# A branch hint over a general path, the flag of that branch written at the end, and a changed warm-up

## The chip, the core and the metric

The kernel runs on one core of a Trainium2 chip. The metric is device time in microseconds (us), lower is better. The core has five engines that run their own instruction streams: TensorE (PE, matmuls, with weight loads PEld listed apart), VectorE (DVE), ScalarE (ACT), GpSimd (POOL) and SyncE (SP), which here issues all DMAs.

## What is computed

Input `x` is 2048 rows of 512 in bf16. Two branches read it and a gate mixes them:

```
g   = sigmoid(sum(x * gate_w))                 # one number per row
q,k,v = x@wq, x@wk, x@wv                       # 32 heads of 16, 4 segments of 512 rows
a_dot = softmax(q k^T / 4 + causal mask) v     # inside a segment
a_mem = phi(q) M / (phi(q) z + 1e-6)           # M, z: sums of phi(k) v and phi(k) of earlier segments
a   = (sigmoid(beta) * a_mem + (1 - sigmoid(beta)) * a_dot) @ wo
b   = (gelu(x @ w_gate) * (x @ w_up)) @ w_down # hidden width 1792
out = g * a + (1 - g) * b
```

## The kernel before

All weights and the transposed x (`xT`) live in SBUF. Work is cut into units that each fill one PSUM bank: four matmuls of 128x512 for a projection (`u_q` L235, `u_k` L290, `u_v` L312, `u_gate` L356, `u_up` L377, `u_out` L409) or fourteen for a down projection (`u_down` L393), followed by one evacuation on VectorE. The attention runs in groups of four heads (`group_qk` L507): four logit matmuls on row tiles of 32 partitions, a ScalarE exponential, GpSimd masks on the diagonal blocks, and then `pv` (L540). The loop over 4 segments, 4 head blocks and 5 groups (L814 to L856) issues one group at a time and fills TensorE with units from queues until a planned time; the order is the one written out by this planner (`manual_schedule`, L575), each engine taking its instructions in program order.

The start: `load_inputs` (L118) issues x0 (the first 512 rows, into a slice of the buffer `G[1]`), then wk, wq, beta, wv and the rest on SP's queue. `warm_up` (L143) clears another slice of `G[1]` and runs nine matmuls of zeros into a bank nobody reads. `transpose_x0` (L149) transposes x0 on TensorE; its copies on VectorE and ScalarE fill `xT`. Then come three k units, four q units, four v units.

The fast path takes the exponential of the logits without subtracting the row maximum. That is safe only while the logits are small. Units `absmax` and `u_bound` (L184, L197) bound them from the largest entries of x, wq and wk; the op at L222 writes `safe`, one int32 that is 1 if the bound holds, in the middle of the run. At the end every engine loads that word into a register (L966) and branches (L967): if it is 0, the block `general()` (L908) computes everything anew with row maxima. With the given inputs `safe` is 1. Of the general block, PE has about 9,300 instructions, DVE 1,336, ACT 677, SP 87, POOL 16. Block order in the program before: the body, the short block of the usual case (each engine waits for its own outstanding work and jumps to the end), the general block, the end. So the usual case falls through the compare and then jumps over the general block. `preferred_fallthrough_block` at L967 decides that order. The `min_val` and `max_val` at L966 make SP also check the value (two short register instructions).

The last step of each segment, `u_out`, adds the two branches into a tile `osb` (L418, three buffers) and SP stores it to `out` (L423). The last segment's four stores are the last DMAs of the kernel. At the end SP waits for all DMA queues, all engines meet at a barrier, semaphores are cleared, and they meet again.

Of the kernel before, what the change touches and what calls it, by code (L numbers as in the profile page):

```python
# [11 lines left out]
ALU = mybir.AluOpType  # L12

P = 128
D = 512
H = 32
DH = 16
NSEG = 4
# [4 lines left out]
EXP_LIMIT = 80.0  # L23
NG = 3
NK = 3
BF = dt.bfloat16
# [18 lines left out]
def kernel(  # L45
# [15 lines left out]
    nc = tc.nc  # L61
# [5 lines left out]
    out2 = out[0]  # L67

    cpool = ctx.enter_context(tc.tile_pool(name="c", bufs=1))
    wk2 = ctx.enter_context(tc.tile_pool(name="wk2", bufs=2))  # L70
# [5 lines left out]
    def const(shape, dtype, name):  # L76
        return cpool.tile(shape, dtype, name=name, tag=name)
# [23 lines left out]
    G = [const([P, HS, L], BF, f"G{i}") for i in range(NG)]  # L101
# [10 lines left out]
    bound = const([1, 8], F32, "bound")  # L112
    safe = const([1, 1], dt.int32, "safe")

    def gen(name):
        return pgen.tile([P, 512], F32, name=name, tag="gen")
# [24 lines left out]
    zero = G[1][:, KT, :]  # L141

    def warm_up():  # L143
        nc.vector.memset(zero, 0.0)
        T = gen("warm")
        for i in range(9):
            nc.tensor.matmul(T[:, :], lhsT=zero[:, 0:P], rhs=zero, start=True, stop=True)

    def transpose_x0():  # L149
        for fc in range(FC):  # L150
            T = pgen.tile([P, 1024], BF, name="x0T", tag="gen")
            for kt in range(KT):
                nc.tensor.transpose(T[:, kt * P:(kt + 1) * P],
                                    x0[:, kt, fc * P:(fc + 1) * P], ident[:, :])
            if fc % 2 == 0:
                nc.vector.tensor_copy(xT[:, fc, 0:L], T[:, 0:512])  # L156
            else:
                nc.scalar.copy(xT[:, fc, 0:L], T[:, 0:512])
# [38 lines left out]
    def u_bound():  # L197
        def join():
            nc.vector.tensor_reduce(out=amax[:, 3:4], in_=amax[:, 3:12], axis=mybir.AxisListType.X,
                                    op=ALU.max)  # L200
            nc.vector.tensor_tensor(out=amax[:, 0:1], in0=amax[:, 0:1], in1=amax[:, 3:4],
                                    op=ALU.max)
            nc.vector.tensor_copy(amaxb[:, :], amax[:, 0:3])
            passed(0.0, 0.3)

        def spread():
            room_for_bank()
            T = gen("bT")
            for i in range(3):
                nc.tensor.matmul(T[0:1, i * P:(i + 1) * P], lhsT=amaxb[:, i:i + 1],  # L210
                                 rhs=ident[:, :], start=True, stop=True)
            nc.vector.tensor_reduce(out=bound[:, 0:3],
                                    in_=T[0:1, 0:3 * P].rearrange("p (i q) -> p i q", i=3),
                                    axis=mybir.AxisListType.X, op=ALU.max)
            passed(0.15, 0.6)

        def test():
            nc.vector.tensor_tensor(out=bound[:, 3:5], in0=bound[:, 1:3],
                                    in1=bound[:, 0:1].to_broadcast((1, 2)), op=ALU.mult)
            nc.vector.tensor_tensor(out=bound[:, 5:6], in0=bound[:, 3:4], in1=bound[:, 4:5],  # L220
                                    op=ALU.mult)
            nc.vector.tensor_scalar(out=safe[:, :], in0=bound[:, 5:6],  # L222
                                    scalar1=float(DH ** 0.5 * D * D), scalar2=EXP_LIMIT,
                                    op0=ALU.mult, op1=ALU.is_le)
            passed(0.0, 0.4)

        def f():
            later(1, join)
            later(3, spread)
            later(5, test)  # L230
        return 0.0, 0.0, f
# [20 lines left out]
    def later(n, f):  # L252
        due.setdefault(clock[0] + n, []).append(f)
# [155 lines left out]
    def u_out(s, qt):  # L409
        def f():  # L410
            T = gen("aT")
            oT = oTs[s]
            for fc in range(FC):
                nc.tensor.matmul(T[:, :], lhsT=oT[:, fc, qt * P:(qt + 1) * P], rhs=wo[:, fc, :],  # L414
                                 start=(fc == 0), stop=(fc == FC - 1))
                if fc < FC - 1:
                    yield MM512
            osb = wk2.tile([P, D], BF, name="osb", tag="osb", bufs=3)  # L418
            nc.vector.scalar_tensor_tensor(out=osb[:, :], in0=T[:, :],
                                           scalar=gct[:, s, qt:qt + 1],  # L420
                                           in1=tBs[(s, qt)][:, :], op0=ALU.mult, op1=ALU.add)
            q0 = s * L + qt * P
            nc.sync.dma_start(out2[q0:q0 + P, :], osb[:, :])  # L423
            return MM512
        return 4 * MM512, EVAC, f

# [149 lines left out]
    load_inputs()  # L576
    make_identity(nc, ident[:, :])
    warm_up()
    transpose_x0()
    setup_consts()  # L580
# [19 lines left out]
    def passed(pe, dve=0.0):  # L600
        backlog[0] = max(0.0, backlog[0] - pe) + dve
        t_pe[0] += pe
# [17 lines left out]
    def room_for_bank():  # L620


        if current:
            current[0][3][0] += 1
            while current and current[0][3][0] > 2:
                step()
# [76 lines left out]
    for i in range(NK, NSEG * NC8):  # L703
        s, c = i // NC8, i % NC8
# [8 lines left out]
    for i in range(NC8, NSEG * NC8):  # L713
        s, c = i // NC8, i % NC8
# [149 lines left out]
    fill_to(1e9)  # L864
    assert not any(st.q for st in streams)


    def phi_now(dst, src):
        e = wk2.tile([P, 2, L], BF, name="phe", tag="phe")
        a = wk2.tile([P, 2, L], BF, name="pha", tag="pha", bufs=1)  # L870
        nc.scalar.activation(e[:, :, :], src, AF.Exp)
        nc.vector.tensor_scalar(out=a[:, :, :], in0=src, scalar1=0.0, scalar2=1.0,
                                op0=ALU.max, op1=ALU.add)
        nc.vector.tensor_tensor(out=dst, in0=e[:, :, :], in1=a[:, :, :], op=ALU.min)
# [88 lines left out]
                for half in range(2):  # L963
                    run(u_M(s, half))

    ok = nc.values_load(safe[0:1, 0:1], min_val=0, max_val=1)  # L966
    with tc.If(ok == 0, preferred_fallthrough_block=False):  # L967
        general()
# [1 line left out]
_INS = ['A_x', 'A_wq', 'A_wk', 'A_wv', 'A_wo', 'A_beta', 'B_x', 'B_w_gate', 'B_w_up', 'B_w_down', 'gate_w']  # L970
# [26 lines left out]
```

## Time and profile before

| what | value |
|---|---|
| time, median of 3 runs | 292.79 us (292.26 to 293.21) |
| profiled execution, its own time | 293.84 us |
| its span in the profile | 292.0 us |
| TensorE busy | 282.9 us, 97% |
| VectorE, ScalarE, GpSimd busy | 74%, 69%, 28% |
| last matmul starts | 286.5 us |
| last output op on VectorE ends | 287.65 us |
| last store: issued, landed | 287.68, 290.39 us |
| barrier after the branch complete | about 291.3 us |

The span runs from the first instruction of the profile to the last. The profiled execution's time is 1.85 us longer than its span; what lies between is ahead of the first recorded instruction or behind the last. A row of the profile's group views gives a source line, an engine (a q behind the name means its sequencer: branches, loads of registers, waits), an operation, how often, shortest, median and longest duration in ns, and first and last start in us.

### The profile page before, as it was taken

To read this page: it belongs to the slowest core of one execution; us is meant where nothing else is said; L and a number is where in the kernel's file an instruction comes from. 1 tells how busy PE (TensorE), PEld (TensorE's weight loads), DVE (VectorE), ACT (ScalarE), POOL (GpSimd) and SP (SyncE) were. 2 spreads that over 40 slices of the span, in tenths; PEclk is the share of its full clock that TensorE was granted. 3 is DMA by queue.
4 is the path that set the end of the run, shared out by engine and by line. 5 is a ranking of instruction groups with operands and counts; after the bars stand their busy time and mean duration, and the time that the engine had idled before them with its cause. 6 is when DMAs were issued, how large, how long until landed. Compare 5 with 4: busy or idle time off the path is not lost.

```text
span 292.0 us, 6916 instructions
## 1 busy us (share of the span) xinstructions
PE 282.9 (97%) x2960; PEld 138.2 (47%) x2960; DVE 215.7 (74%) x422; ACT 200.7 (69%) x125; POOL 82.7 (28%) x140
## 2 busy tenths in 40 slices
PE   7899999999999999999999999999999999999992
PEld 4344445554444454545444454455544544544451
DVE  1788488777876869987878968988768567785453
ACT  3226877768897776776898785767748968777600
POOL 4000043344204334243410424242323033244300
PEclk9999999999999999999999999999999999999998
DMA  6989940200000000400000001033101000011002
GB/s 214 325 189 251 308 84 3 54 20 2 20 0 2 20 20 18 93 20 20 18 20 18 2 2 36 3 76 34 38 0 38 2 0 20 18 21 38 22 19 79
DMA packets 29444, 15.85 MB, mean 54 GB/s; under 512 B 21984, under 2 KB 28384, under 8 KB 29408
## 3 DMA queue, kind: packets, MB, share of 16 engines
q1 hardware_dynamic: 29408, 15.35, 21.0%
q8 instruction: 25, 0.41, 0.6%
q14 instruction: 11, 0.09, 0.1%
HBM read 8.14 MB, written 2.10 MB: 35 GB/s over the span
## 4 chain that ended last, share of the span: by engine, by line
PE 56%; DVE 3%; issue 0%; DVEq 0%
PE dT L397 14%; PE uT L381 10%; PE od L546 7%; PE gT L360 6%; PE lg L519 6%; PE aT L414 4%; PE kT L294 2%; PE vT L316 2%; PE qT L239 2%; PE mn L496 1%; PE MT L434 1%; DVE ktb L299 0%; DVE G L368 0%; DVE pha L271 0%; DVE o L556 0%
## 5 line engine op out<-in xcount | busy, mean ns | idle before, releaser
L525 ACT ACTIVATE pT<-lg 128x2048 bf16<-128x2048 f32 x80 | 150.1, 1876 | 57.1 <-PE lg L519 46.0
L536 POOL TENSOR_SCALAR_AFFINE_SELECT pT<-pT 128x512 bf16<-128x512 bf16 x128 | 79.5, 639 | 194.1 <-ACT pT L525 192.2
L381 PE MATMUL uT<-xT,wup 128*128 128x512 bf16 x224 | 62.3, 379 | 0.0
L360 PE MATMUL gT<-xT,wga 128*128 128x512 bf16 x224 | 60.2, 379 | 0.6 <-DVE G L368 0.4
L397 PE MATMUL dT<-wdn,G 128*128 128x512 bf16 x224 | 55.2, 379 | 0.2 <-DVE G L387 0.2
L546 PEld LDWEIGHTS <-pT 128*128 128x128 bf16 x1280 | 43.6, 96 | 17.7 <-issue 0.4
L546 PE MATMUL od<-V,pT 128*128 128x17 bf16 x1280 | 43.9, 170 | 0.0
L387 DVE TENSOR_TENSOR G<-uT,G 128x512 bf16<-128x512 f32 x56 | 38.3, 686 | 6.8 <-PE uT L381 6.4
L368 DVE CAST G<-gT 128x512 bf16<-128x512 f32 x42 | 28.8, 685 | 8.0 <-PE gT L360 7.7
L519 PE MATMUL lg<-QT,KT 32*128 32x384 bf16 (+3 forms) x512 | 31.7, 301 | 0.0
L360 PEld LDWEIGHTS <-wga 128*128 128x128 bf16 x224 | 19.7, 97 | 22.8 <-issue 5.5
L397 PEld LDWEIGHTS <-G 128*128 128x128 bf16 x224 | 19.5, 97 | 22.2 <-issue 3.9
L381 PEld LDWEIGHTS <-wup 128*128 128x128 bf16 x224 | 19.2, 97 | 20.8 <-issue 5.0
L402 DVE TENSOR_SCALAR tB<-dT,omg 128x512 bf16<-128x512 f32 x16 | 12.0, 750 | 19.9 <-PE dT L397 19.8
L519 PEld LDWEIGHTS <-KT 32*128 32x128 bf16 x512 | 8.9, 92 | 29.8 <-issue 29.5
L375 ACT ACTIVATE G<-G 128x3584 bf16<-128x3584 bf16 x6 | 18.8, 3182 | 0.0
L239 PE MATMUL qT<-xT,wq 128*128 128x512 bf16 x64 | 17.4, 379 | 1.1 <-DMA wq<-in_A_wq_dram 1.1
L552 DVE RECIPROCAL rden<-od 128x16 f32<-128x16 f32 x32 | 8.2, 256 | 13.7 <-PE od L546 13.4
L294 PE MATMUL kT<-xT,wk 128*128 128x512 bf16 x64 | 17.1, 380 | 0.3 <-DVE xT L156 0.3
L414 PE MATMUL aT<-wo,oT 128*128 128x512 bf16 x64 | 16.4, 379 | 0.5 <-DVE G L368 0.5
L316 PE MATMUL vT<-wv,xT 128*128 128x512 bf16 x64 | 16.4, 380 | 0.0
L366 ACT ACTIVATE G<-gT 128x512 bf16<-128x512 f32 x14 | 8.4, 598 | 9.7 <-PE gT L360 9.7
(81 smaller groups left out, 226.2 us busy)
## 6 DMA issues: line engine op xcount, KB each, us to landing
out_dram<-osb SPq DMA_DIRECT2D x16, 128.0 KB, 1.7
wga<-in_B_w_gate_dram SPq DMA_DIRECT2D x1, 1792.0 KB, 13.7
wup<-in_B_w_up_dram SPq DMA_DIRECT2D x1, 1792.0 KB, 8.7
wdn<-in_B_w_down_dram SPq DMA_DIRECT2D x1, 1792.0 KB, 10.3
G<-in_A_x_dram SPq DMA_DIRECT2D x1, 512.0 KB, 3.9
wk<-in_A_wk_dram SPq DMA_DIRECT2D x1, 512.0 KB, 4.8
wq<-in_A_wq_dram SPq DMA_DIRECT2D x1, 512.0 KB, 9.0
wv<-in_A_wv_dram SPq DMA_DIRECT2D x1, 512.0 KB, 9.7
```

The source lines that it names most:

```text
L239: nc.tensor.matmul(T[:, :], lhsT=wq[:, fc, c * P:(c + 1) * P], rhs=xT[:, fc, s * L:(s + 1) * L], start=(fc == 0), stop=(fc == FC - 1))
L294: nc.tensor.matmul(T[:, :], lhsT=wk[:, fc, c * P:(c + 1) * P], rhs=xT[:, fc, s * L:(s + 1) * L], start=(fc == 0), stop=(fc == FC - 1))
L360: nc.tensor.matmul(T[:, :], lhsT=wga[:, fc, hs * P:(hs + 1) * P], rhs=xT[:, fc, s * L:(s + 1) * L], start=(fc == 0), stop=(fc == FC - 1))
L368: nc.vector.tensor_copy(G[s % NG][:, hs, :], T[:, :])
L381: nc.tensor.matmul(T[:, :], lhsT=wup[:, fc, hs * P:(hs + 1) * P], rhs=xT[:, fc, s * L:(s + 1) * L], start=(fc == 0), stop=(fc == FC - 1))
L387: nc.vector.tensor_tensor(out=g, in0=T[:, :], in1=g, op=ALU.mult)
L397: nc.tensor.matmul(T[:, :], lhsT=G[s % NG][:, hs, qt * P:(qt + 1) * P], rhs=wdn[:, hs, :], start=(hs == 0), stop=(hs == HS - 1))
L414: nc.tensor.matmul(T[:, :], lhsT=oT[:, fc, qt * P:(qt + 1) * P], rhs=wo[:, fc, :], start=(fc == 0), stop=(fc == FC - 1))
L519: nc.tensor.matmul(lg[:, j, off:off + n], lhsT=KTm[pp][32 * j:32 * j + 32, (NC8 * s + c) % NK, kt * P:(kt + 1) * P], rhs=QT[32 * j:32 * j ...
L525: nc.scalar.activation(pT[:, :, :], lg[:, :, :], AF.Exp, scale=DH ** -0.5)
L536: nc.gpsimd.affine_select(out=v, in_=v, pattern=pat, compare_op=ALU.is_ge, fill=0.0, base=0, channel_multiplier=-1)
L546: nc.tensor.matmul(od[:, qq, j, 0:17], lhsT=t[:, j, o:o + P], rhs=V[s % 2][:, kt, 8 * c + 2 * j + p, 0:17], start=(kt == 0), stop=(kt == qq))
```

## The change

Four edits. (1) `tc.If` gets a label and lets the general block fall through, and the usual block is moved behind it; a branch hint "LikelyTaken" for that branch is given to TensorE, VectorE and ScalarE. In the built program the hint is one instruction on each of the three, at the very start of the body, ahead of the first zero matmul. SP and GpSimd have the same branch without a hint. (2) The op that writes `safe` goes from `u_bound` to the end of the body; in VectorE's stream it stands right behind the last segment's last output op. The value check on SP goes. (3) The last segment's `osb` is a slice of `G[1]` in place of a tile of the three-buffer pool, so those four ops do not wait for earlier stores. (4) The nine zero matmuls become six, followed by eight of 256 columns on column tiles of 32. TensorE's body has 11 instructions more (ten for the warm-up, one hint); otherwise each engine's order is as before.

```diff
     def warm_up():
         nc.vector.memset(zero, 0.0)
         T = gen("warm")
-        for i in range(9):
+        for i in range(6):
             nc.tensor.matmul(T[:, :], lhsT=zero[:, 0:P], rhs=zero, start=True, stop=True)
+
+        for i in range(8):
+            j = i % 4
+            nc.tensor.matmul(T[32 * j:32 * j + 32, 0:256], lhsT=zero[:, 32 * j:32 * j + 32],
+                             rhs=zero[:, 0:256], start=True, stop=True,
+                             tile_position=(0, 32 * j))
...
-            nc.vector.tensor_scalar(out=safe[:, :], in0=bound[:, 5:6],
-                                    scalar1=float(DH ** 0.5 * D * D), scalar2=EXP_LIMIT,
-                                    op0=ALU.mult, op1=ALU.is_le)
             passed(0.0, 0.4)
...
-            osb = wk2.tile([P, D], BF, name="osb", tag="osb", bufs=3)
-            nc.vector.scalar_tensor_tensor(out=osb[:, :], in0=T[:, :],
+            if s == NSEG - 1:
+
+                osb = G[(s + 1) % NG][:, qt, :]
+            else:
+                osb = wk2.tile([P, D], BF, name="osb", tag="osb", bufs=3)[:, :]
+            nc.vector.scalar_tensor_tensor(out=osb, in0=T[:, :],
...
-            nc.sync.dma_start(out2[q0:q0 + P, :], osb[:, :])
+            nc.sync.dma_start(out2[q0:q0 + P, :], osb)
...
+    tc.mark_branch_hint_location("safe", "LikelyTaken",
+                                 [mybir.EngineType.PE, mybir.EngineType.DVE,
+                                  mybir.EngineType.Activation])
...
-    ok = nc.values_load(safe[0:1, 0:1], min_val=0, max_val=1)
-    with tc.If(ok == 0, preferred_fallthrough_block=False):
+    nc.vector.tensor_scalar(out=safe[:, :], in0=bound[:, 5:6],
+                            scalar1=float(DH ** 0.5 * D * D), scalar2=EXP_LIMIT,
+                            op0=ALU.mult, op1=ALU.is_le)
+    ok = nc.values_load(safe[0:1, 0:1])
+    with tc.If(ok == 0, preferred_fallthrough_block=True, label="safe"):
         general()
```

## The prediction

> **What bounds the kernel now.** I read the page first (share of each engine), then the page's DMA part, then the views of lines 966, 967, 992 and 423, and last the timeline of TensorE's start.
>
> ```profile
> span 292.0 us, 6916 instructions
> PE 282.9 (97%) x2960; PEld 138.2 (47%) x2960; DVE 215.7 (74%) x422; ACT 200.7 (69%) x125; POOL 82.7 (28%) x140
> ...
> q8 instruction: 25, 0.41, 0.6%
> ...
> out_dram<-osb SPq DMA_DIRECT2D x16, 128.0 KB, 1.7
> ```
>
> TensorE is busy 97% of the span, so the body is TensorE's. The change touches only what lies before its first projection and after its last matmul (286.9 us). Queue q8 moved 25 packets of instructions, 16 KB each (0.41 MB / 25). From 286.9 to 292.0 no engine needs matmuls; that stretch is the branch. The views of lines 967, 966, 992 and 423, one row per engine (count, min/median/max ns, first and last start in us):
>
> ```profile
> L967 ACTq COMPARE_BRANCH  x2: 38/44/49, 275.0 to 276.4; - x2
> L967 POOLq COMPARE_BRANCH  x2: 38/42/45, 276.9 to 277.7; - x2
> L967 PEldq COMPARE_BRANCH  x2: 83/1806/3530, 285.7 to 287.1; - x2
> L967 DVEq COMPARE_BRANCH  x2: 51/53/55, 287.6 to 287.8; - x2
> L967 SPq COMPARE_BRANCH  x2: 38/48/57, 288.9 to 290.5; - x2
> ```
> ```profile
> L966 PEldq TENSOR_LOAD <-safe x1: 484/484/484, 285.1 to 285.1; - x1
> L966 DVEq TENSOR_LOAD <-safe x1: 546/546/546, 286.9 to 286.9; - x1
> L966 SPq TENSOR_LOAD <-safe x1: 498/498/498, 288.1 to 288.1; - x1
> ```
> ```profile
> L992 SPq DRAIN  x3: 7/7/13, 291.2 to 291.5; - x3
> L992 ACTq DRAIN  x2: 8/54/100, 278.9 to 291.5; - x2
> L992 PEldq DRAIN  x2: 8/40/73, 290.6 to 291.6; - x2
> L992 DVEq DRAIN  x2: 10/34/59, 290.9 to 291.5; - x2
> ```
> ```profile
> DMA to landing us min/median/max: 1.7/1.7/2.7
> ```
>
> The second COMPARE_BRANCH of each engine is its jump over the general path; its DRAIN at line 992 is the first instruction behind the jump. PE leaves at 287.05 and arrives at 290.64 (3.59 us), DVE at 287.79 and 290.92 (3.13), ACT at 276.42 and 278.94 (2.5). POOL and SP, whose general blocks are 16 and 87 instructions, need under 0.2. So three engines stall in the jump. The trace's transfer records show why: a 16 KB instruction packet starts at 288.23 and takes 0.92 us; 8 KB ones start at 277.3 and 289.06.
>
> The end barrier waits for the last to arrive: by semaphore events PE 290.73, DVE 290.99, **SP 291.26**. SP ends last, and for another reason: it waits for the last output. That DMA was issued at 287.68 and landed at 290.385, 2.70 us later, where the median is 1.7 (line above). Fifteen of its sixteen semaphore counts came by 289.62, fourteen of them by 289.38. The sixteenth belongs to eight packets of 1 KB that ran one after another from 289.14 to 289.90: one DMA engine, starting as the 16 KB instruction packet ended (288.23 + 0.92 = 289.15). So TensorE's stall costs through a collision with the last store, more than by itself. From the landing SP takes 0.88 to arrive, then the barriers 0.72 to 291.985.
>
> **The change, part by part.** The sum is made against the profiled execution: span 291.985, its own time 293.84, which is 1.05 over the median of the runs, 292.79. I carry the difference over.
>
> *Hint and order of blocks.* General code now falls through and the usual path is the taken branch, with a hint for PE, DVE and ACT. If a target is fetched while the body still runs, the stalls go and with them the packet at 288.23. Landing: 287.683 + 1.69 (issue to landing of the two stores before the collision: 285.09 to 286.78, 285.95 to 287.64) = 289.38, against 290.385: **-1.0 us**. If the fifteenth count, at 289.62, stays where it is: -0.77. I take -0.98, nearer the row of the undisturbed stores. SP's 0.88 and 0.72 behind it are unchanged; next to be late is SP itself, still.
>
> *Flag written last.* The op costs 142 ns (its row, at 189.3 us) and moves behind the last output op, which ends at 287.655. Flag there at about 287.83. Every engine's load of it (0.47 to 0.55) now waits for that: behind it on PE, ACT, DVE and POOL there is only the branch; on SP too, whose load starts at 288.07 anyway, since it issues the last store first. Loads end near 288.4, branches near 288.5; then an own-engine wait, a second branch and the drain, 0.3: PE, DVE, ACT and POOL arrive near 289, 1.2 us ahead of SP's 289.38 + 0.88 = 290.26. Cost 0. If a fetch still comes then, that cover is gone (first rival). POOL and SP have no hint; their targets are as near as before (16 and 87 instructions): 0. SP's two register instructions (0.19 and 0.02) go: it waits for the landing anyway, 0.
>
> *A new fetch.* Each jump is followed by a fetch of the next block 0.59 to 0.67 us after the drain starts (PE 290.64 and 291.315, DVE 290.92 and 291.505, ACT 278.94 and 279.556). With jumps near 288.5 these fall near 289.1 to 289.25; the last store's packets end at 289.03 on undisturbed DMA engines. It clears, by 0.1 to 0.2 us: second rival.
>
> *Last outputs into G.* The last segment's four ops no longer wait for a store to free osb. The fourth did wait: for a landing at 286.783, but TensorE's result came later (286.875). Gain 0, covered by 0.09. G's slice was last read long before: 0.
>
> *Zero matmuls.* The start, in order of time (start, length, idle before):
>
> ```profile
> 4.22 1.06 PE L147 MATMUL warm<-G 128*128 128x512 bf16 x2
> 5.07 1.69 PE L153 MATMUL x0T<-ident,G 128*128 128x128 bf16 x16
> 7.05 2.75 PE L294 MATMUL kT<-xT,wk 128*128 128x512 bf16 x12 [0.29 <-DVE xT L156]
> 10.95 1.47 PE L239 MATMUL qT<-xT,wq 128*128 128x512 bf16 x6 [1.15 <-DMA wq<-in_A_wq_dram]
> ```
>
> The nine zero matmuls start 0.427 apart; x0 has landed by 4.67, so the transposes start 0.36 later than they could. Six end at 1.3 + 6 x 0.427 = 3.86. Eight of 256 columns: one by one 8 x 0.213 = 1.71, or, if four column tiles run beside each other as the four row tiles of line 519 do (four matmuls of 512 columns in 0.39), 0.43. No row shows column tiles; I take 0.43. Transposes then start between 4.7 and 5.6, i.e. -0.35 to +0.5 against 5.07. The 1.15 us that TensorE waits for wq at 10.95 swallows all of it: **0**. In a run where wq lands earlier, up to -0.3 comes through. The hints themselves are three instructions at the start, some 0.05 each by the branches' rows, under the same cover.
>
> Sum: -0.98. Span 291.0, profiled time 292.86, median **291.8**; the forecast's own range is 291.4 (-0.98 and -0.3 from the start) to 292.05 (-0.77).
>
> **Rivals.**
> 1. *The hint does nothing; slower.* It stands some 5,960 TensorE instructions ahead of its branch. For it: no row shows a hint at work. Against: a block is fetched long before it is run (TensorE's last one ahead of the branch at 276.3, 10.8 us before its jump), so there is time in which the target could be fetched too. Then the late flag puts the fetch at the very end: PE branches at 288.47, drains 3.59 + 0.15 later at 292.2, arrives 292.3, end + 0.72 = 293.0, +1.03: **293.8**. It decides as soon as a stall exceeds 291.26 - 288.7 = 2.5 us; DVE's and PE's do. The Trainium skill speaks for this one: Runtime: NRT & Kernel Launch, Instruction fetch mechanics, says that prefetch is purely sequential and a taken branch out of the window forces a fetch. The trace agrees with the second half (3.59 us); on the first nothing here tells, and by it the time would be this rival's.
> 2. *The stalls go, the landing stays late.* The target's or the next block's fetch meets the last store after all: 0.2 us earlier than I put it and one DMA engine's last packets wait up to 0.92. Gain 0.06 to 0.4: **292.6**. For it: the fetch of 16 KB did this at 288.23. Against: the margin above. If the landing was late for another reason, the change doesn't do what it says: 292.8, counted here.
> 3. *The clock comes late.* Transposes run 107 ns apart at first and 56 from 6.4 us: full rate came there. With a gap before x0 and narrow tiles in place of full ones, it may come only after kT: 12 x 0.427 = 5.12 in place of 2.75, kT ends 1.2 us past 10.95. Net +0.2: **293.0**. If it comes at 9.8, kT ends near 10.9 and nothing is lost; that is why I hold it unlikely. The Trainium skill, TensorE: Matmul & The Clock Gate, Part 1 and Part 4, says that the clock is released after a busy window of some 3.4 us and that transposes do not count as busy, which speaks for it; the order of events here (1.3 to 6.4) does not contradict either half.
>
> **How the numbers follow.** Forecast 0.60, rival 1 0.18, rival 2 0.13, rival 3 0.09. 0.3% is 0.88 us, about what a measurement of this kernel can tell from no change. Most of the forecast lies beyond it (0.50), gains of 0.77 to 0.88 do not (0.10). Rival 2 is within; rival 3 mostly (0.06, else 0.03 slower); rival 1 mostly slower (0.16, 0.02 within). Faster 0.50, same 0.31, slower 0.19. The range runs from 291.3 to 293.1: it takes in rivals 2 and 3 and leaves out rival 1's 0.18.
>
> **What would show it.** Right: PE's and DVE's branch near 288.5 followed by a drain within 0.4 us; the last store landing 1.7 us after issue; SP last to the barrier near 290.3; no 16 KB instruction packet between 287 and 289; first qT matmul still waiting for wq near 10.9. Wrong: a branch of over 2 us after 288.4 (rival 1); prompt drains but a landing over 2.2 us (rival 2); kT matmuls 0.427 apart, or qT after 11.2 without waiting for wq (rival 3).

## The result and the profile after

The changed kernel takes 291.29 us (median of 6 runs, 290.84 to 291.66); the kernel before, run beside it, 292.94 (6 runs, 292.26 to 293.21). The ratio is 0.9946, 95% interval 0.993 to 0.9961: 1.65 us faster, where 0.98 was forecast. That is at the low edge of the stated range (291.3 to 293.1) and below the forecast's own range (291.4 to 292.05). Two more measurements of the same kernel, shown below, gave 0.9938 each.

The page of the profile after (own time 291.33, span 289.4), the lines that answer to those shown of before:

```profile
span 289.4 us, 6869 instructions
...
q8 instruction: 24, 0.39, 0.6%
...
out_dram<-osb SPq DMA_DIRECT2D x12, 128.0 KB, 1.7
```

(The page counts fewer instructions than before, although TensorE's body has eleven more: some fifty matmul records are missing from this trace, 2915 against 2965 weight loads.) There is one 16 KB instruction packet fewer. By the trace's transfer records the last three stood at 276.3, 288.2 and 291.3 us before, the second 1.18 us behind the start of TensorE's jump; the last two now stand at 274.9 and 288.1. The one at 288.1 starts 0.5 us behind TensorE's drain, so TensorE did not wait for it. Up to 277 us both kernels have 23 such packets: no record shows when the hinted block was loaded. The views of line 981 (branches), 1006 (behind the jump, and the hints at the start) and 430 (stores):

```profile
L981 ACTq COMPARE_BRANCH  x1: 68/68/68, 286.9 to 286.9; - x1
...
L981 PEldq COMPARE_BRANCH  x1: 411/411/411, 287.0 to 287.0; - x1
L981 DVEq COMPARE_BRANCH  x1: 84/84/84, 287.0 to 287.0; - x1
...
L981 SPq COMPARE_BRANCH  x1: 53/53/53, 287.3 to 287.3; - x1
```
```profile
L1006 SPq DRAIN  x3: 7/7/13, 288.6 to 289.0; - x3
...
L1006 PEldq DRAIN  x2: 8/8/8, 287.6 to 289.0; - x2
L1006 DVEq DRAIN  x2: 10/14/17, 287.8 to 289.0; - x2
...
L1006 PEldq BRANCH_PREFETCH_HINT  x1: 50/50/50, 0.9 to 0.9; - x1
```
```profile
DMA to landing us min/median/max: 1.7/1.7/2.0
```

TensorE's branch takes 0.41 us in place of 3.53, and its drain follows 0.6 us behind the branch's start. VectorE's takes 0.73 from branch to drain in place of 3.1. The last store lands 1.70 us after its issue (by the semaphore counts 286.35 to 288.05) in place of 2.70 (the 2.0 of the view is an earlier store), and SP is last at the barrier, at 288.72.

A measure that leaves out all that happens earlier is the **end**: from the end of the last output op on VectorE to the end of the span. It was 287.65 to 291.99 = 4.33 us before and is 286.33 to 289.44 = 3.11 now. The two spans differ by more, 2.55 us, but 1.33 of that lies ahead of the last output op, and most of it is chance in the one execution, as the experiments show. TensorE's start after (start, length, idle before):

```profile
1.34 2.74 PE L147 MATMUL warm<-G 128*128 128x512 bf16 x6 [1.34 <-DVE G L144]
4.01 0.62 PE L151 MATMUL warm<-G 128*32 128x256 bf16 x8
4.93 1.50 PE L159 MATMUL x0T<-ident,G 128*128 128x128 bf16 x16 [0.30 <-DMA G<-in_A_x_dram]
6.67 2.75 PE L297 MATMUL kT<-xT,wk 128*128 128x512 bf16 x12 [0.23 <-DVE xT L162]
9.26 2.75 PE L242 MATMUL qT<-xT,wq 128*128 128x512 bf16 x11
```

The wait for wq ahead of the qT matmuls is gone: wq landed at 8.57 us, before the kT matmuls were through, where it landed at 10.90 in the profile before.

### The profile page after: what moved, and what is told of

It is laid out like the page before. It is cut to its first block, busy times and chain, and to the rows that moved or that the text cites. A ratio compares the mean times of both kernels' runs of the same rounds, so it can differ in the third digit from the quotient of the medians.

```text
span 289.4 us, 6869 instructions
## 1 busy us (share of the span) xinstructions
PE 277.4 (96%) x2915; PEld 137.7 (48%) x2965; DVE 215.5 (74%) x422; ACT 200.7 (69%) x125; POOL 82.7 (29%) x140
## 4 chain that ended last, share of the span: by engine, by line
PE 56%; DVE 3%; issue 1%; DVEq 0%
PE dT L400 14%; PE uT L384 10%; PE od L553 7%; PE gT L363 6%; PE lg L526 6%; PE aT L417 4%; PE kT L297 2%; PE vT L319 2%; PE qT L242 2%; PE mn L503 1%; PE MT L441 1%; DVE ktb L302 0%; DVE G L371 0%; DVE pha L274 0%; DVE o L563 0%
## 5 line engine op out<-in xcount | busy, mean ns | idle before, releaser
L384 PE MATMUL uT<-xT,wup 128*128 128x512 bf16 x208 | 59.5, 379 | 1.3 <-issue 0.6
L363 PE MATMUL gT<-xT,wga 128*128 128x512 bf16 x211 | 57.0, 379 | 1.0 <-DVE G L371 0.4
L400 PE MATMUL dT<-wdn,G 128*128 128x512 bf16 x212 | 53.2, 379 | 1.1 <-issue 0.3
L242 PE MATMUL qT<-xT,wq 128*128 128x512 bf16 x57 | 16.2, 379 | 0.5 <-DVE QT L247 0.2
```

The lines of the kernel that those rows point to most:

```text
L363: nc.tensor.matmul(T[:, :], lhsT=wga[:, fc, hs * P:(hs + 1) * P], rhs=xT[:, fc, s * L:(s + 1) * L], start=(fc == 0), stop=(fc == FC - 1))
L384: nc.tensor.matmul(T[:, :], lhsT=wup[:, fc, hs * P:(hs + 1) * P], rhs=xT[:, fc, s * L:(s + 1) * L], start=(fc == 0), stop=(fc == FC - 1))
L400: nc.tensor.matmul(T[:, :], lhsT=G[s % NG][:, hs, qt * P:(qt + 1) * P], rhs=wdn[:, hs, :], start=(hs == 0), stop=(hs == HS - 1))
```

## The experiments

Theory A: the end is shorter by some 1.2 us since the targets are fetched ahead, and the start adds what wq's wait hid. Theory B, as predicted: the start adds nothing. Rivals about the parts: the block order alone does it, the flag's place doesn't matter, the stores from G matter.

**The new warm-up alone** (label e1). The kernel before with:

```diff
-        for i in range(9):
+        for i in range(6):
             nc.tensor.matmul(T[:, :], lhsT=zero[:, 0:P], rhs=zero, start=True, stop=True)
+        for i in range(8):
+            j = i % 4
+            nc.tensor.matmul(T[32 * j:32 * j + 32, 0:256], ..., tile_position=(0, 32 * j))
```

> The kernel before with the new warm-up alone (six full zero matmuls and eight on column tiles). Theory A: the start is worth time in most runs, because wq usually lands before TensorE has done its k units (8.6 us in the profile after; 10.9 us in the profile before was an exception): 0.4 us faster than before, about 292.5. Theory B, the prediction's: TensorE waits for wq anyway, so nothing: 292.9. In the profile, A wants the first qT matmul right behind the last kT matmul, near 9.3 us, B wants it waiting for wq near 10.9.

Measured: 292.75 (12 runs) against 292.76, ratio 1.0 (0.9983 to 1.0017), as B has it, to half a microsecond. Its profile fits neither: wq landed at 9.54 and the first qT matmul, idle for 0.41 us, waited for it until 9.58. The end is 4.60 us, the last store landing 2.97 us after issue: the old end, longer than in the profile before.

**All but the warm-up** (e2, and once more as e10). The changed kernel with:

```diff
-        for i in range(6):
+        for i in range(9):
             nc.tensor.matmul(T[:, :], lhsT=zero[:, 0:P], rhs=zero, start=True, stop=True)
-        for i in range(8):
-            ...
```

> The changed kernel with the nine full zero matmuls of before, so the hint, the order of blocks, the late flag and the stores from G alone. Theory A: the end alone is worth 1.2 us (last output op to end of span 4.33 us before, 3.11 after): 291.7. Theory B: the end is worth all of the measured 1.65 us: 291.3.

Measured: 291.73 (12 runs) against 292.76, ratio 0.9964 (0.9947 to 0.9981). The end is 3.12 us. So by the medians the end makes 1.0 us (0.6 to 1.6) of the 1.65 (1.1 to 2.1); the intervals overlap.

**Without the hint** (e3). The changed kernel with:

```diff
-    tc.mark_branch_hint_location("safe", "LikelyTaken",
-                                 [mybir.EngineType.PE, mybir.EngineType.DVE,
-                                  mybir.EngineType.Activation])
```

> The changed kernel without the three hint instructions. Theory A (the hint moves the fetch of the target): the jumps stall again, now behind the late flag. TensorE's branch takes about 3.5 us and it is last at the barrier; last output op to end of span about 4.33 + 1.0 = 5.4 us in place of 3.1, so about 2.2 us over the changed kernel: 293.5. Rival (the order of the blocks or the late flag took the stall away, not the hint): no branch over 0.5 us and 291.3.

Measured: 294.28 (8 runs) against 292.76, ratio 1.0056 (1.0034 to 1.0078): slower than before. The end is 5.74 us. The views of the branch line and of the lines behind it:

```profile
L977 PEldq COMPARE_BRANCH  x1: 4004/4004/4004, 286.9 to 286.9; - x1
L977 DVEq COMPARE_BRANCH  x1: 72/72/72, 287.0 to 287.0; - x1
```
```profile
L1002 ACTq DRAIN  x2: 8/8/9, 289.7 to 291.5; - x2
L1002 DVEq DRAIN  x2: 10/14/17, 290.3 to 291.5; - x2
L1002 PEldq DRAIN  x2: 8/8/8, 291.2 to 291.6; - x2
```

All three stalls are back, behind the late flag, and TensorE's is last. The last store still lands in 1.70 us, since the fetch (at 288.4) now comes after it. The hint is what removes the stall, and this kernel is what the first rival of the prediction described: its price was put at +1.03 over before and is +1.5.

**The flag early, with the hint** (e4). The changed kernel with:

```diff
+            nc.vector.tensor_scalar(out=safe[:, :], in0=bound[:, 5:6], ...)   # back in u_bound
             passed(0.0, 0.4)
...
-    nc.vector.tensor_scalar(out=safe[:, :], in0=bound[:, 5:6], ...)           # ahead of the branch
```

> The changed kernel with the flag written in the middle of the run, as before; hint and block order as in the changed kernel. Theory A (what TensorE fetches behind its jump meets the last store): TensorE jumps right after its last matmul, 1.5 us earlier than with the late flag, its next 16 KB fetch starts about 0.65 us later, when the last store is under way, and one DMA engine's packets of that store wait: landing up to 0.5 us later, 291.3 to 291.8. Rival (the place of the flag doesn't matter once the target is there): 291.3, last store landing 1.7 us after its issue.

Measured: 292.61 (12 runs) against 292.76, ratio 0.9996 (0.998 to 1.0013). The end is 3.91 us. No engine stalls in the jump, and yet nearly all of the gain is lost: 0.80 us of it at the end, and perhaps more to a late clock, which this profile has (below). TensorE's branch, and the stores, last segment and all:

```profile
L981 PEldq COMPARE_BRANCH  x1: 406/406/406, 285.8 to 285.8; - x1
...
L433 SPq DMA_DIRECT2D out_dram<-G x4: 332/332/991, 285.2 to 287.8; - x4
...
DMA to landing us min/median/max: 1.7/1.7/3.5
```

TensorE's branch ends at 286.2, its drain stands at 287.1, right behind its last matmuls, and its next 16 KB fetch starts at 287.05 and takes 1.3 us, among the stores. Semaphore counts: fifteen of the second store's sixteen come by 287.72, the last at 289.56; of the third, fifteen by 288.60, the last at 289.87. Even SP's issue of the fourth store takes 0.99 us in place of 0.33, and there the end loses most: that store is the last to land, 2.49 us after its issue began in place of 1.70, and 0.66 of these 0.79 us are the issue. Why the issue is slow is not shown. The expected 0.5 us was too little: three stores are hit, not one.

**The flag early, without the hint** (e12). The changed kernel with the edits of e3 and e4 both.

> The new block order and the stores from G with the flag in the middle of the run and no hint. Theory A: TensorE's sequencer takes the branch while its last matmuls run, so its stall of 3.5 to 4 us starts near 285.8 and ends near 289.7, hidden but for the fetch, which meets the last stores; VectorE's stall of 3.1 us starts near 287.7 and makes it arrive near 291: 292.9, about as before. Rival (without a hint the order alone helps): 291.7.

Measured: 292.07 (10 runs) against 292.69, ratio 0.9971 (0.9956 to 0.9986), between theory and rival. The end is 3.93 us.

```profile
L977 PEldq COMPARE_BRANCH  x1: 3987/3987/3987, 284.6 to 284.6; - x1
L977 DVEq COMPARE_BRANCH  x1: 72/72/72, 286.4 to 286.4; - x1
```

TensorE stalls 4 us, but from 284.6 on, while its queued matmuls run, so it drains at 288.8, ahead of SP. What is left is the fetch at 285.6 among the stores and, as in e4, a slow issue of the fourth (0.93 us): the same end to 0.02 us. By the end, the hint is worth nothing with an early flag; with a late one it is worth 2.6 us (5.74 against 3.11). The block order seems to have a part of its own: with neither hint nor late flag this kernel is 0.6 us (0.4 to 1.3) faster than before, while the new warm-up alone gave nothing (e1). In the kernel before TensorE jumped only after its last matmuls (at 287.05); here it jumps at the compare, ahead of their end.

**The hint on TensorE alone** (e8).

```diff
-                                 [mybir.EngineType.PE, mybir.EngineType.DVE,
-                                  mybir.EngineType.Activation])
+                                 [mybir.EngineType.PE])
```

> The changed kernel with the hint on TensorE alone. Theory A (each engine's stall stands by itself and the last one to the barrier counts): VectorE's jump takes 3.2 us behind the late flag and VectorE is last, its drain near 4.0 us after the last output op; last output op to end of span 4.8 us in place of 3.1, so 293.0. Rival (only TensorE's 16 KB fetch costs, by its collision with the store): 291.4.

Measured: 293.43 (10 runs) against 292.96, ratio 1.0014 (0.9991 to 1.0037). The end is 4.85 us, as theory A has it:

```profile
L1005 PEldq DRAIN  x2: 8/8/8, 289.2 to 292.4; - x2
L1005 ACTq DRAIN  x2: 8/8/9, 291.5 to 292.3; - x2
L1005 DVEq DRAIN  x2: 10/14/17, 291.9 to 292.3; - x2
```

TensorE is there at 289.2; ScalarE and VectorE, 2.9 and 3.2 us behind their branches, at 291.5 and 291.9. So the hint on TensorE takes away TensorE's stall only. ScalarE, 3.5 us behind the last output op, would still be later than SP, which arrived 2.4 us behind it in the changed kernel; so by these rows all three hints are needed, though no kernel with two was run.

**The last outputs from the pool** (e7).

```diff
-            if s == NSEG - 1:
-                osb = G[(s + 1) % NG][:, qt, :]
-            else:
-                osb = wk2.tile([P, D], BF, name="osb", tag="osb", bufs=3)[:, :]
+            osb = wk2.tile([P, D], BF, name="osb", tag="osb", bufs=3)[:, :]
```

> The changed kernel with the last segment's outputs in the three-buffer pool, as before. Theory A: no difference, since the fourth op's wait for a landing ends 0.09 us before TensorE's result. Rival (stores from the slice of G matter): 0.1 to 0.9 us slower, and a wait of VectorE for a DMA ahead of its last output op.

Measured: 291.63 (10 runs) against 292.96, ratio 0.9953 (0.9934 to 0.9973), not clear of the changed kernel's 0.9938 on the same chip (291.35). The end is 3.11 us, and the last output op starts 0.87 us behind the one before it, as the others do. No effect found.

**The changed kernel again** (e5, e11) **and nine full zero matmuls again** (e10).

> The changed kernel itself once more, beside the next three. The kernel with the end alone measured 1.0 us under before, the warm-up alone 0.0, the changed kernel 1.65. Theory A: the end is worth 1.2 us (last output op to end of span 4.33 before, 3.11 after) and the rest of the 1.65 is the spread of the start: 291.6 here. Theory B: the warm-up adds 0.4 to 0.6 where the end is short: 291.2 again.

> The changed kernel beside the one with nine full zero matmuls: 291.3 if its first two measurements are typical; one execution in seven or so 1.3 us longer if the clock sometimes comes one period later with the new warm-up, as it did in the profiles of three kernels that share it.

> The end alone with nine full zero matmuls, once more, beside the changed kernel on the same chip. If the new warm-up is worth something where the end is short, this kernel is 0.3 to 0.6 us slower than the changed one; if the end is all, they agree within 0.2 us.

Measured: 291.35 (7 runs) against 292.96, ratio 0.9938 (0.9916 to 0.996), and 290.95 (6 runs) against 292.69, ratio 0.9938 (0.9916 to 0.9959). With nine full matmuls 291.82 (12 runs), ratio 0.9961 (0.9946 to 0.9975). All 19 executions of the changed kernel lie between 290.84 and 291.66, so none was 1.3 us longer; the 24 with nine full matmuls lie between 290.78 and 293.08, medians 291.05 and 291.79. The end is 3.12 us in the profiles of both. So beside the short end the new warm-up looks worth 0.4 to 0.9 us, where alone it was worth nothing measurable; the intervals overlap. Nor do the profiles show it: the last output op ended at 285.8 to 286.5 us in the three of the changed kernel and at 286.0 and 286.3 in the two with nine full matmuls. Its share is **not settled**.

**Six full zero matmuls alone** (e6). The changed kernel with:

```diff
         for i in range(6):
             nc.tensor.matmul(T[:, :], lhsT=zero[:, 0:P], rhs=zero, start=True, stop=True)
-        for i in range(8):
-            ...
```

> The changed kernel with the eight matmuls on column tiles left out, six full zero matmuls alone. Theory A (the start is set by when x0 and wq land and by when the clock is granted, not by what fills the gap): the same as the changed kernel within 0.5 us. Rival (the column tiles keep TensorE busy for the clock): full rate comes later, k matmuls 0.427 us apart for up to 3 us, 0.5 to 1.3 us over the changed kernel.

Measured: 292.68 (12 runs) against 292.96, ratio 0.9989 (0.9972 to 1.0007): 1.3 us over the changed kernel, as the rival has it. One of the twelve took 291.07, the others 292.40 to 293.04. TensorE's start in its profile:

```profile
4.86 1.89 PE L153 MATMUL x0T<-ident,G 128*128 128x128 bf16 x16 [0.78 <-DMA G<-in_A_x_dram]
6.84 3.98 PE L291 MATMUL kT<-xT,wk 128*128 128x512 bf16 x12
10.66 1.68 PE L236 MATMUL qT<-xT,wq 128*128 128x512 bf16 x7
```

The kT matmuls take 3.98 us in place of 2.75 and run 0.427 apart until full rate is granted at 9.36 us. The end is 3.12: nothing but the start differs. So the column tiles are no filler; they are worth 1.3 us against leaving the gap empty.

**The kernel before, profiled again** (e9).

> The kernel before, profiled once more. Theory: the first qT matmul's wait for wq until 10.9 us was that execution's alone (wq landed between 7.8 and 9.7 us in seven later profiles of the variants), so here wq lands before 10 us and the last output op ends earlier than 287.65; the end (last output op to end of span) is again 4.3 to 4.6 us, with the last store landing 2.7 to 3.0 us after its issue. Rival: the kernel before makes wq late (10.9 again).

One run, 292.83. wq landed at 7.71, and the last output op ended at 286.19, earlier than in the profile after. The end is 4.80 us. Its branch line, stores and start:

```profile
L967 PEldq COMPARE_BRANCH  x2: 83/2006/3930, 284.3 to 285.6; - x2
```
```profile
DMA to landing us min/median/max: 1.7/1.7/3.2
```
```profile
5.07 1.38 PE L153 MATMUL x0T<-ident,G 128*128 128x128 bf16 x16
6.52 2.75 PE L294 MATMUL kT<-xT,wk 128*128 128x512 bf16 x12
9.11 2.75 PE L239 MATMUL qT<-xT,wq 128*128 128x512 bf16 x12
```

The wait for wq that the prediction leaned on is not there. The old end varies with how long TensorE's fetch takes: 4.33, 4.60 and 4.80 us in three profiles (before, e1, e9), the last store landing 2.70, 2.97 and 3.17 us after its issue, where the 16 KB packet behind the jump took 0.92, 1.16 and 1.33. The new end is 3.11 to 3.12 in seven.

## Why the prediction was right, and where it was off

*Hint and block order: right in what it does.* With the hint the branches are short (e3 has the stalls back), and the last store lands 1.7 us after issue, as in a store that nothing disturbs. The -1.0 us for the landing is exact against the profile it was made from; against the other two profiles of the old end it would be -1.3 and -1.5. The term was taken from the mildest of three. That the target is fetched while the body still runs, the condition of this term, is not shown: the records have no packet for it.

*"SP's 0.88 and 0.72 behind it are unchanged": wrong by 0.21.* From landing to SP's arrival it takes 0.67 now (288.05 to 288.72); the 0.72 held. SP used to jump over the general block after the landing; with the new order it jumps at the compare, and behind the landing only the next instruction follows. By its records, the wait that ends at the landing is followed 0.26 us later by the next one before (290.402 to 290.658), 0.07 now (288.068 to 288.134). The prediction counted SP's jump as a cost nobody had, since it did not stall; but it stood on the path.

*Flag written last: right that it costs nothing, and too modest.* It is the condition for the last 0.8 us of the end: e4 and e12 have an end of 3.9 us, and TensorE's fetches then fall among the stores. Behind the jump there is a fetch all the same, of the next block by its place. With the late flag the first 8 KB packet comes at 288.01 and TensorE's 16 KB at 288.12, 0.3 and 0.4 us after the last store's packets end (287.70). That is a wider margin than the 0.1 to 0.2 that I gave it; the hinted jump still takes 0.6 us to the drain.

*Stores from G: right*, no effect in e7.

*Zero matmuls, 0: its cover was one execution's.* "The 1.15 us that TensorE waits for wq at 10.95 swallows all of it": wq landed between 7.6 and 9.7 us in thirteen other profiles, and only in one of them (e1, 0.41 us) did TensorE wait for it to speak of. So an earlier start does come through to the k units. Transposes begin at 4.72 to 4.93 in the profiles of the changed kernel against 5.07 to 5.16 in three of the four with nine full matmuls (in the fourth, e2, the clock came at 4.40 and let the zero matmuls finish early); kT begins at 6.18 to 6.67 against 6.38 to 7.05, some 0.3 us earlier. That is the -0.3 that the text held open. What it is worth in the median stays open, as said above. The eight narrow matmuls took 0.62 us, where I took 0.43 from row tiles.

*Rivals.* The first is e3. Its threshold was off, though: with the late flag the store lands undisturbed (1.70 us in e3), so by the prediction's own 290.26 for SP a stall of 1.6 us would already have decided, not 2.5. The second has its mechanism in e4: with a fetch among the stores the end is 0.8 us longer. The third is real: full rate came at 9.7 to 10.4 us in three of nine profiles that share the new warm-up (e4, e7, e8), though in none of the changed kernel itself, and then the last output op ended at 287.7 to 288.0 instead of 285.8 to 286.7. The text held this unlikely; it is the largest effect here that varies from execution to execution. It goes with the landing of x0: in these three x0 landed at 5.08 to 5.23 us and TensorE stood idle for 0.49 to 0.69 us ahead of the transposes (e4: 0.64). In the other six x0 landed at 4.65 to 4.89 and the gap was at most 0.36 (0.30 in the row shown of the changed kernel). e6, with a gap of 0.78 by its edit, has the late clock too. So the gap is the likely trigger, and the new warm-up leaves one whenever x0 is late; no run varied the landing alone. With nine full matmuls none of four profiles had the late clock, nor did x0 land after 4.87 in any of them.

So the sum was off in two terms: the end, forecast -0.98 and measured -1.22 between the first two profiles (1.00 by the landing, 0.21 by SP) and -1.2 to -1.7 over all, and the start, forecast 0 and left open by the runs. That the result still touches the low edge of the range is near to luck: nothing in the sum reaches 291.29. (The ends of the forecast's own range, redone, are 291.5 and 292.0.)

Three of the signs named for being right did not come as written: VectorE's drain comes 0.7 us behind its branch, not within 0.4; there is a 16 KB packet between 287 and 289 us, at 288.12, which no one waits for; and the qT matmuls do not wait for wq. Two did: the landing after 1.70 us, and SP last at the barrier.

The Trainium skill, Runtime: NRT & Kernel Launch, Instruction fetch mechanics, was cited for the first rival. The stall that it tells of is there without a hint (e3, 4.0 us); with one the branch takes 0.41 us, and there the measurement decides. The Trainium skill, TensorE: Matmul & The Clock Gate, Part 1, gives a free-running window of about 3.4 us: full rate came between 4.40 and 6.38 us in ten profiles and between 9.36 and 10.44 in four, and the stretch at full rate lasted 283.31 us in each of the ten and 279.89 in each of the four, 3.41 us less, which agrees.

## What to carry to other kernels

Behind the last matmul, look at what the instruction queues fetch: here a jump over a large block stalled its engine for 2.5 to 4.2 us, and TensorE's 16 KB packet held up the last store. A hint per engine takes the stall away, but that paid only with the branch placed so that the next fetch falls after the last store's packets. Hint and place are one edit: the hint with the early branch gained nothing measurable, the late branch without the hint lost 1.5 us. Take no cover from a wait for a DMA that one profile shows: profile the same kernel twice.

## What the runs showed of the hardware

- The hint, given 286 us and about 5,960 instructions ahead, still worked. It costs 45 to 51 ns once.
- Eight matmuls on column tiles: the first four start within 10 ns of each other (4.015 to 4.025), the next four 0.19 us later; eight took 0.62 us.
- A 16 KB instruction packet behind the last branch took 0.9 to 1.5 us. Where one fell among the stores, the last of a store's sixteen semaphore counts came up to 1.8 us late (e4, second store).
- With the same program start full rate was granted at 4.4 us in one execution and at 10.4 in another. The last output op ended 1.0 to 2.2 us later in the three late profiles than in the six others.
